# A planned attention and gated feed-forward kernel: GpSimd may take squares and weight sums, the planner's durations are set anew, and every engine gets a new order

## The chip, the cores and the metric

The program runs on one core of a Trainium2 chip. A core has five engines with a queue each: TensorE (PE in the profile, with its weight loads as PEld), VectorE (DVE), ScalarE (ACT), GpSimd (POOL) and SyncE (SP), which here only issues transfers. Each engine takes its instructions strictly in the order in which they were written and starts one only when the semaphores that it waits for have been raised. The metric is the device time of one execution in microseconds (us), median of three: 1039.81 us (1039.11 to 1039.89).

## The reference

Attention with random features, for 8 batches of 8 heads, 576 tokens and 64 dimensions, 128 features, followed by a gated feed-forward layer on 4608 tokens of 512 dimensions, 1536 hidden. Cut to what is computed:

```python
q_s, k_s = q * scale, k * scale
def phi(x):
    h = einsum('bhsd,md->bhsm', x, omega) - sum(x * x, -1, keepdims=True) / 2
    return exp(h - max(h, -1, keepdims=True)) / sqrt(m)
q_p, k_p = phi(q_s), phi(k_s)
kv, z = einsum('bhsm,bhsd->bhmd', k_p, v), sum(k_p, axis=2)
num, den = einsum('bhsm,bhmd->bhsd', q_p, kv), einsum('bhsm,bhm->bhs', q_p, z) + 1e-6
x = (num / den) laid out as (tokens, heads * dims)
out = ((x @ w_a) * (x @ w_b)) @ w_out
```

## The kernel before

Two heads of one batch make a unit; 8 batches of 4 units are 32 units, named in the tiles as batch and pair (`hk_0_1` belongs to batch 0, pair 1). A unit's scores are matmuls of the inputs with omega (L583 for four chunks of 128 tokens, L603 for eight), a row maximum on VectorE (L654, L613), the squares of the inputs and their row sums (`square_sums`: the square at L564, the sum at L569, tiles `natk` and `natq`, result `sq`), two small VectorE instructions that make the bias (L661 and L662) and eight exponentials on ScalarE for each of `hk` and `hq` (L667, L623). In batch 0 the chunks are then transposed on TensorE (L990), multiplied with `kv` (L1013, L1027) and divided (L1032 to L1039) to `x32t` and, turned once more (L1046), to `x`. From batch 1 on the sum over keys, `z`, is added up on GpSimd in six instructions (L829 in `z_sums`), finished on VectorE (L845 to L856), written to memory and read back to all partitions as `zb`; `hq` is divided by it (L895 to L911), turned on VectorE (L918) and through memory, and goes into the numerator `pm` (L950).

The feed-forward layer works block by block, one batch (512 of its tokens) a block, over twelve slices of the hidden dimension. Every value is split into a high and a low part, so a product is three matmuls. In blocks 0 and 1 (`moe_block`) a slice is 12 matmuls into `pa` and 12 into `pb` (L1285), a copy of `pa` to `a` on ScalarE, the product `a` times `pb` on VectorE (L1293), its split into `ghl` (L400 or L402, then L408), and 12 matmuls into the four output banks (L1093). There are two PSUM banks for `pa` and `pb`, so the next slice's `pb` waits for the product of this one. From block 2 on (`moe_block7`, L1383) two slices go together with seven products of half matrices in place of eight. These need sums of quarters of the weights, which `weight_sums` makes once, between the first slice of block 1 and the start of block 2: for each of 6 slice pairs and both weights two adds `wr` (L1317), one subtraction of 128x512 (L1326) and two of 128x256 (L1323, tile `tf`), then their split into `ts` and its transfer to memory. The weights come as 64 bit numbers; three instructions (L450, L452 on ScalarE, L454 on VectorE) and a split (L400 or L402, L408) turn 36 tiles `raw` into high and low parts, in the stretch from about 28 to 171 us.

The order of all work is made by a planner (`Graph`) when the program is built. Each piece of work (`op`) has the engines that may do it, each with a duration in ns, what it reads and writes, and a priority. `run` lays the pieces out in time by these durations, choosing an engine where there is a choice; `dues` works back from the last piece of TensorE to a due time for each; and for each list in `CHOSEN` the layout is made again by due times, with a seed for each 15 us of planned time that shifts due times by random amounts (`shifted`). What is written into each queue is that last order. The durations decide nothing on the chip by themselves; only the order and the choice of engines get into the program. Two rules of the planner's time belong to the change: `PORT` lengthens a VectorE piece that lies beside a GpSimd piece (L284), unless the piece is exempt (`o.port`), and `TURNS` adds a pause where TensorE goes from one kind of matmul to another (`mode`).

In batch 0 the inputs of units 1 to 3 have their squares made on ScalarE (unit 0 has another way, L638 to L643). The weight sums are VectorE's alone.

Of the kernel before, what the change touches and what calls it, by code (L numbers as in the profile page):

```python
# [61 lines left out]
class Graph:  # L62
# [4 lines left out]
    TURNS = {"fr": 190, "rf": 205, "fc": 145, "cf": 205, "rc": 250, "cr": 250}  # L67
# [292 lines left out]
def tile_attention_moe(ctx: ExitStack, tc: tile.TileContext, kqt, kqtt, kqn, kqnt, vx, omst, idn, wab, wout, out):  # L360
# [200 lines left out]
    def square_sums(src, sq, n, nm, pr, b, alloc_sq):  # L561

        for nat, o, part in src:
            s = g.op({"ACT": act(n * D)}, lambda e, nat=nat: nc.scalar.activation(nat.ap[:], nat.ap[:], AF.Square, scale=SQ) if e == "ACT" else  # L564
                     nc.gpsimd.tensor_tensor(nat.ap[:], nat.ap[:], nat.ap[:], op=ALU.mult),
                     r=[(nat, None)], w=[(nat, None)], prio=pr, margin=0 if b < 2 else CFG["LOAD"])
# [1043 lines left out]
```

## Time and profile before

| what | value |
|---|---|
| median of three runs | 1039.81 us |
| the profiled execution's own time | 1038.92 us |
| its span on the core | 1037.1 us |
| PE busy | 1020.0 us (98%) |
| DVE busy | 803.8 us (78%) |
| ACT busy | 635.5 us (61%) |
| POOL busy | 117.2 us (11%) |
| granted clock of TensorE | 0.999 |
| HBM | 302 GB/s over the span |

The share of an engine over the whole span hides stages. In the first 13 us the inputs arrive; until about 50 us the four units of batch 0 run; blocks 0 and 1 of the feed-forward layer with the units of batches 1 to 3 fill the time to 300 us; then the blocks with seven products run to the end, until about 780 us with units beside them. A time of one group of instructions is a mean or a median over the profiled execution. PE counts as busy while a matmul is in its pipeline, so a short pause of TensorE shows in PEld (weight loads) rather than in PE.

### The profile page before, as it was taken

Reading aid. Unit: us, or ns where it says so; the run is one execution under the profiler, and the core shown is the slowest. Engines: PE = TensorE matmul, PEld = TensorE weight load, DVE = VectorE, ACT = ScalarE, POOL = GpSimd, SP = SyncE. Lnnn points to the kernel's source line nnn. Section 1 sums busy time; section 2 is a strip of 40 time slices with the busy share of each in tenths; the row PEclk is TensorE's granted clock in tenths of the full one; section 3 lists DMA queues with packets and bytes.
Section 4 is the critical chain, followed back from the end, with each engine's and each line's share of the span. In section 5 each row is a group of like instructions: output and inputs, shape, how many; then the busy total and the mean of one; then the engine's idle time right before and its main releaser. Section 6 shows DMA issues by size and latency. Waiting matters only on the chain.

```text
span 1037.1 us, 25617 instructions
## 1 busy us (share of the span) xinstructions
PE 1020.0 (98%) x9902; PEld 895.7 (86%) x9902; DVE 803.8 (78%) x1580; ACT 635.5 (61%) x1690; POOL 117.2 (11%) x181
## 2 busy tenths in 40 slices
PE   8899999999999999999999999999999999999998
PEld 6677777777788898989898889988989899999997
DVE  6999999999987687676776868677757467887545
ACT  7998787777676575667556666675555234444322
POOL 0133111111111111110201111111110000000000
PEclk9999999999999999999999999999999999999999
DMA  9977878999889898879898998988798899999991
GB/s 358 335 250 247 291 236 266 323 335 332 292 296 387 301 319 299 319 278 368 283 321 301 340 304 296 363 287 315 249 303 265 267 316 337 334 326 358 338 336 56
DMA packets 123658, 314.39 MB, mean 303 GB/s; under 512 B 17680, under 2 KB 40976, under 8 KB 123536
## 3 DMA queue, kind: packets, MB, share of 16 engines
q1 hardware_dynamic: 122656, 312.10, 86.6%
q8 instruction: 78, 1.28, 0.5%
q10 hardware_dynamic: 880, 0.66, 0.2%
q14 instruction: 44, 0.36, 0.1%
HBM read 255.52 MB, written 57.18 MB: 302 GB/s over the span
## 4 chain that ended last, share of the span: by engine, by line
PE 82%; DVE 12%; ACT 4%; issue 1%; DMA 1%; SPq 0%; DVEq 0%; ACTq 0%
PE p L1383 41%; PE o L1093 19%; PE o_P L1163 5%; PE pa L1285 3%; PE pb L1285 3%; PE pkv L876 3%; PE pm L950 2%; DVE sm L654 2%; PE ppk L603 2%; PE p L603 1%; DVE raw L454 1%; PE p L1163 1%; ACT hq L667 1%; DMA zb<-zdr 1%; ACT hk L667 1%
## 5 line engine op out<-in xcount | busy, mean ns | idle before, releaser
L1093 PE MATMUL o<-wo,ghl 128*128 128x512 f32 x1008 | 263.2, 396 | 0.4 <-DVE ghl L408 0.4
L1093 PEld LDWEIGHTS o<-wo,ghl 128*128 128x128 f32 x1008 | 178.6, 188 | 36.3 <-issue 4.1
L400 ACT COPY c<-p 128x512 f32<-128x512 f32 x150 | 87.4, 583 | 145.7 <-PE p L1383 137.8
L1395 DVE TENSOR_TENSOR c<-p,c 128x512 f32<-128x512 f32 x144 | 98.6, 685 | 71.1 <-PE p L1383 36.4
L1383 PE MATMUL p<-Sa,t 128*128 128x256 f32 x1008 | 133.4, 280 | 0.0
L1383 PEld LDWEIGHTS p<-Sa,t 128*128 128x128 f32 x1008 | 126.2, 188 | 2.3 <-issue 0.2
L829 POOL TENSOR_TENSOR z<-hk 128x256 f32<-128x256 f32 x56 | 48.0, 856 | 601.4 <-ACT hk L623 402.8
L1459 DVE TENSOR_TENSOR c<-c 128x512 f32<-128x512 f32 x82 | 57.8, 707 | 40.1 <-ACT c L400 39.4
L911 ACT ACTIVATE hq<-hq,dn 128x128 f32<-128x128 f32 x224 | 69.3, 390 | 13.5 <-DVE dn L907 13.0
L1285 PE MATMUL pa<-x,wa 128*128 128x512 f32 x288 | 74.4, 400 | 2.1 <-ACT a L400 1.1
L1285 PE MATMUL pb<-x,wb 128*128 128x512 f32 x288 | 72.3, 397 | 1.5 <-DVE a L1293 1.5
L1383 PE MATMUL p<-x,wa 128*128 128x256 f32 x504 | 73.7, 282 | 0.0
L1383 PE MATMUL p<-x,wb 128*128 128x256 f32 x504 | 73.2, 281 | 0.0
L1383 PEld LDWEIGHTS p<-x,wa 128*128 128x128 f32 x504 | 67.2, 188 | 3.3 <-ACT hk L400 0.6
L1383 PE MATMUL p<-Sb,t 128*128 128x256 f32 x504 | 68.4, 283 | 0.0
L1383 PEld LDWEIGHTS p<-x,t 128*128 128x128 f32 x504 | 64.7, 189 | 2.6
L1285 PEld LDWEIGHTS pa<-x,wa 128*128 128x128 f32 x288 | 52.6, 188 | 16.4 <-ACT a L400 1.9
L1383 PE MATMUL p<-Sb,bq 128*128 128x256 f32 x504 | 66.8, 282 | 0.0
L1285 PEld LDWEIGHTS pb<-x,wb 128*128 128x128 f32 x288 | 53.3, 188 | 15.5 <-DVE a L1293 2.8
L1383 PE MATMUL p<-x,t 128*128 128x256 f32 x504 | 66.7, 281 | 0.0
L1383 PEld LDWEIGHTS p<-Sb,bq 128*128 128x128 f32 x504 | 64.3, 189 | 2.4
L1383 PEld LDWEIGHTS p<-x,wb 128*128 128x128 f32 x504 | 65.4, 188 | 0.1
(217 smaller groups left out, 1983.9 us busy)
## 6 DMA issues: line engine op xcount, KB each, us to landing
t<-td SPq DMA_DIRECT2D x168, 512.0 KB
wo<-wod SPq DMA_DIRECT2D x96, 512.0 KB
bq<-bd SPq DMA_DIRECT2D x84, 256.0 KB
qdr<-qd SPq DMA_DIRECT2D x112, 160.0 KB
hq<-qdr SPq DMA_DIRECT2D x28, 640.0 KB
X<-in_kqt_dram SPq DMA_DIRECT2D x30, 512.0 KB
raw<-in_wab_dram SPq DMA_DIRECT2D x24, 512.0 KB
td<-ts SPq DMA_DIRECT2D x24, 512.0 KB
```

The source lines that it names most:

```text
L400: nc.scalar.copy(o(), i())
L603: nc.tensor.matmul(flat[c // 4][w]()[half, c % 4 * M:c % 4 * M + M], x()[rows, c * P + D * t:c * P + D * t + D], om.ap[rows], start=True, ...
L654: g.op({"DVE": dve(4 * M)}, lambda e, w=w, whole=whole: nc.vector.tensor_reduce(sm.ap[:, 0, w, sl], whole(), axis=X, op=ALU.max), r=held[w ...
L829: g.op({"POOL": pool2(n)}, lambda e: nc.gpsimd.tensor_tensor(o(), a(), c(), op=ALU.add), r=r, w=w, alloc=list(al), prio=pri, deps=zload[-1 ...
L876: nc.tensor.matmul(pkv.ap[D * j + d:D * j + d + Q, 0:M], vb.ap[:, vc, d:d + Q], c(), start=(n == 0), stop=(n == 4))
L911: g.op({"ACT": 392}, lambda e, c=c, src=src: nc.scalar.activation(hq.ap[:, c], src(), AF.Copy, scale=dn.ap[:, c:c + 1]), r=[sd, (dn, None) ...
L1093: nc.tensor.matmul(po.ap[:], ghl.ap[:, gi, t * P:(t + 1) * P], wo.ap[:, wi], start=(n == 0 and i == 0), stop=(n == NF - 1 and i == 2))
L1163: nc.tensor.matmul(pb.ap[:, t], A[0](ai)[:, t * P:(t + 1) * P], W[0](wi), start=begin and t == j == 0, stop=stop and t == 1 and j == 2)
L1285: nc.tensor.matmul(pb.ap[:], wt.ap[:, wi, c], xs[c].at(xi), start=(c == 0 and i == 0), stop=(c == NC4 - 1 and i == 2))
L1383: nc.tensor.matmul(pb.ap[:, w], W[w][0](wi, c), X[0](xi, c), start=fresh and n == w == 0, stop=n == 5, skip_group_check=True)
L1395: g.op({"DVE": dve(SM)}, lambda e: nc.vector.tensor_tensor(o.ap[:, q], pb.ap[:], C[y[0]].ap[:, y[1]], op=ALU.add), r=[(pb, 0), (pb, 1), (C ...
L1459: g.op({"DVE": dve(SM)}, lambda e, c=C[k]: nc.vector.tensor_tensor(c.ap[:, :, 1], c.ap[:, :, 1], c.ap[:, :, 0], op=ALU.mult), r=part, w=pa ...
```

## The change

`square_sums` lets GpSimd make the square in batch 0; where it does, the factor 0.5/8 that ScalarE puts into the square is applied by one more small VectorE instruction after the row sum. `weight_sums` lets GpSimd make each of the five sums. The other edits are to the planner's durations: `PORT` goes from 0.5 to 0.4, pieces that read one tensor or reduce are exempt from it (`port=False`), the pauses in `TURNS` become shorter and get a kind `h` for the two small matmul groups of `tok_tail`, whose durations go from 2200 to 1200 and from 1100 to 610, and the two instructions of the division there become one piece. `CHOSEN` holds another list of seeds, 17 long instead of 8: seeds now act in planned time from 15 to 30 us, 195 to 210 us and 240 to 255 us.

```diff
-    TURNS = {"fr": 190, "rf": 205, "fc": 145, "cf": 205, "rc": 250, "cr": 250}
+    TURNS = {"fr": 90, "rf": 150, "fc": 90, "cf": 145, "rc": 170, "cr": 170, "fh": 95, "hf": 125, "rh": 170, "hr": 125, "hc": 150, "ch": 150}
...
-        o.port = not any(b.ring in ("at", "ab", "o") for b, _ in r)
+        o.port = port and not any(b.ring in ("at", "ab", "o") for b, _ in r)
+        if not o.port and "ACT" in eng and any(b.ring in ("at", "ab", "o") for b, _ in r):
+            o.any = eng = dict(eng, ACT=eng["ACT"] - 30)
...
-            s = g.op({"ACT": act(n * D)}, lambda e, nat=nat: nc.scalar.activation(nat.ap[:], nat.ap[:], AF.Square, scale=SQ) if e == "ACT" else
-                     nc.gpsimd.tensor_tensor(nat.ap[:], nat.ap[:], nat.ap[:], op=ALU.mult),
+            s = g.op({"ACT": act(n * D) + 25, **({"POOL": pool2(n * D)} if b == 0 else {})}, lambda e, nat=nat: nc.scalar.activation(nat.ap[:], nat.ap[:], AF.Square, scale=SQ) if e == "ACT" else
+                 nc.gpsimd.tensor_tensor(nat.ap[:], nat.ap[:], nat.ap[:], op=ALU.mult),
...
                 if "POOL" in s.eng:
-                    nc.gpsimd.tensor_scalar(o(), o(), SQ2, 0.0, op0=ALU.mult, op1=ALU.add)
+                    nc.vector.tensor_scalar(o(), o(), SQ2, None, op0=ALU.mult)
...
-            g.op({"DVE": dve(SM)}, lambda e, k=k, v=v: nc.vector.tensor_tensor(wr.ap[:, k], v(0), v(1), op=ALU.add),
+            g.op({"DVE": dve(SM), "POOL": pool2(SM)}, lambda e, k=k, v=v: ENG[e].tensor_tensor(wr.ap[:, k], v(0), v(1), op=ALU.add),
...
-            g.op({"DVE": dve(HM)}, lambda e: nc.vector.tensor_tensor(t[k](), x(), y(), op=ALU.subtract),
+            g.op({"DVE": dve(HM), "POOL": pool2(HM)}, lambda e: ENG[e].tensor_tensor(t[k](), x(), y(), op=ALU.subtract),
...
-        g.op({"DVE": dve(SM)}, lambda e: nc.vector.tensor_tensor(tf.ap[:, 1:3], wr.ap[:, 1].rearrange("p (h n) -> p h n", n=HM), wr.ap[:, :, 0:HM],
+        g.op({"DVE": dve(SM), "POOL": pool2(SM)}, lambda e: ENG[e].tensor_tensor(tf.ap[:, 1:3], wr.ap[:, 1].rearrange("p (h n) -> p h n", n=HM), wr.ap[:, :, 0:HM],
```

Counted over the built programs, TensorE has the same instructions in another order, and goes from one kind of matmul to another 170 times, before 168 times. All six squares of batch 0 go from ScalarE to GpSimd, with six small VectorE instructions (L573 in the changed kernel) more. Of the 60 weight sums 24 go to GpSimd: nine `wr`, three `tf` of 128x512 and twelve `tf` of 128x256. Of the casts and copies that either engine may make, VectorE has 79 instead of 83.

Three places in the order matter. The first is ScalarE's queue from the last exponentials of unit 0 to the first ones of unit 1 (`hk_0_1`, `hq_0_1`). Before:

```order
L667 ACTIVATE hq_0_0_182<-ppq_0_04_240,sm_0_0_183 128x128 x4
L564 ACTIVATE natk_0_1_157<-natk_0_1_157 128x512
L667 ACTIVATE htk_0_0_210<-ppke_0_00_208,sme_0_0_212 128x128
L400 COPY kvz_0_0_331<-pkv_0_0_330 128x132
L667 ACTIVATE htk_0_0_210<-ppke_0_00_208,sme_0_0_212 128x128
L564 ACTIVATE natq_0_1_159<-natq_0_1_159 128x512
L400 COPY qT_0_0_320<-pq_0_02_366 128x384
L667 ACTIVATE htq_0_0_211<-ppqe_0_00_209,sme_0_0_212 128x128 x3
L564 ACTIVATE natk_0_2_165<-natk_0_2_165 128x512
L564 ACTIVATE natq_0_2_167<-natq_0_2_167 128x512
L564 ACTIVATE natk_0_3_173<-natk_0_3_173 128x512
L667 ACTIVATE hq_0_1_296<-ppq_0_14_375,sm_0_1_297 128x128 x4
```

The same stretch of ScalarE's queue in the changed kernel:

```order
L669 ACTIVATE hq_0_0_182<-ppq_0_04_240,sm_0_0_183 128x128 x4
L669 ACTIVATE htk_0_0_210<-ppke_0_00_208,sme_0_0_212 128x128 x3
L402 COPY kvz_0_0_340<-pkv_0_0_339 128x132
L669 ACTIVATE hk_0_1_296<-ppk_0_10_294,sm_0_1_298 128x128 x2
L402 COPY qT_0_0_324<-pq_0_02_380 128x384
L669 ACTIVATE hk_0_1_296<-ppk_0_10_294,sm_0_1_298 128x128
L669 ACTIVATE hq_0_1_297<-ppq_0_10_295,sm_0_1_298 128x128
```

Five squares stood ahead of unit 1's first exponential; now none does, and it follows the copy of `kvz` directly. The second place is GpSimd's queue from its start. Before:

```order
L424 MEMSET zw_70 128x32
L1018 MEMSET tails_0_1_483 64x128
L1018 MEMSET tails_0_2_730 64x128
L1018 MEMSET tails_0_3_840 64x128
L829 ISA
L829 TENSOR_TENSOR z2_1_0_993<-hk_1_0_913 128x256
```

GpSimd's queue from its start in the changed kernel:

```order
L426 MEMSET zw_70 128x32
L567 ISA
L567 TENSOR_TENSOR natk_0_1_157<-natk_0_1_157 128x512
L567 TENSOR_TENSOR natq_0_1_159<-natq_0_1_159 128x512
L567 TENSOR_TENSOR natk_0_2_165<-natk_0_2_165 128x512
L567 TENSOR_TENSOR natq_0_2_167<-natq_0_2_167 128x512
L567 TENSOR_TENSOR natk_0_3_173<-natk_0_3_173 128x512
L567 TENSOR_TENSOR natq_0_3_175<-natq_0_3_175 128x512
L1020 MEMSET tails_0_1_564 64x128
```

The six squares, and with them the configuring instruction that precedes GpSimd's first `TENSOR_TENSOR` (shown as `ISA`), moved ahead of everything that waits for batch 0's results. The third place is GpSimd's queue at the first slice of block 1, between the `z` sums of units 2_1 and 2_2, in the changed kernel (before, the `z` sums follow each other there):

```order
L831 TENSOR_TENSOR zs_2_1_2458<-z2_2_1_2457 128x128
L831 TENSOR_TENSOR zs_2_1_2458<-zs_2_1_2458,htk2_2145 64x128
L1328 TENSOR_TENSOR tf00_2721<-wr00_2636 128x512
L1325 TENSOR_TENSOR tf00_2721<-wr00_2636,tf00_2721 128x256
L1319 TENSOR_TENSOR wr01_2760<-wb1_1099 128x512
L831 TENSOR_TENSOR z2_2_2_2809<-hk_2_2_2614 128x256
L831 TENSOR_TENSOR zs_2_2_2810<-z2_2_2_2809 128x128
```

Three weight sums now stand ahead of unit 2_2's `z` sum in the same queue.

## Rows read from the trace of the kernel before

**Rows 1.** Busy time by stage: the stretch, its length, busy us and instructions (x) of each engine, TensorE's granted clock, the busy share of the transfer engines, GB/s.

```profile
0.00:13.00 13.00, 11.51 (x193) 8.58 (x195) 6.35 (x16) 7.33 (x21) 0.94 (x10) 1.00 0.84 304
13.00:46.00 33.00, 26.80 (x552) 21.99 (x549) 30.26 (x81) 32.81 (x99) 1.30 (x3) 1.00 0.98 378
...
60.00:165.00 105.00, 103.61 (x903) 79.61 (x896) 103.72 (x212) 91.42 (x242) 22.67 (x25) 1.00 0.77 253
165.00:300.00 135.00, 133.15 (x1144) 102.81 (x1143) 130.55 (x252) 97.53 (x265) 25.23 (x36) 1.00 0.93 319
300.00:780.00 480.00, 480.00 (x4958) 429.10 (x4959) 348.19 (x661) 303.42 (x841) 61.87 (x102) 1.00 0.89 311
```

**Rows 2.** What TensorE's weight loads waited for from 165 to 300 us, longest first: who waits, for whom, us in total, times, longest.

```profile
PEld pkv L952 <- issue: 3.6, 12, 0.3
PEld pa L1285 <- ACT a L400: 1.9, 2, 1.3
PEld pkv L876 <- issue: 1.8, 5, 0.4
PEld pb L1285 <- DVE a L1293: 0.9, 1, 0.9
```

**Rows 3.** The timeline of ScalarE, 13.6 to 18 us and at the last split of batch 0's `x`: start us, length us, engine, line, operation, tiles.

```profile
13.62 0.77 ACT L564 ACTIVATE natk<-natk 128x512 f32<-128x512 f32 x1
...
16.44 0.83 ACT L564 ACTIVATE natk<-natk 128x512 f32<-128x512 f32 x1
16.95 0.83 ACT L564 ACTIVATE natq<-natq 128x512 f32<-128x512 f32 x1
17.48 0.83 ACT L564 ACTIVATE natk<-natk 128x512 f32<-128x512 f32 x1
18.00 1.33 ACT L667 ACTIVATE hq<-ppq,sm 128x128 f32<-128x128 f32 x4
19.02 1.35 ACT L667 ACTIVATE hk<-ppk,sm 128x128 f32<-128x128 f32 x4
...
45.71 0.59 ACT L400 CAST x<-px 128x512 fp32r<-128x512 f32 x1
```

**Rows 4.** The timeline of VectorE around unit 1's first row sum, with the idle time before an instruction and who ended it; then around the first product of block 0 (`a<-pb,a`).

```profile
11.18 0.69 DVE L654 TENSOR_REDUCE sm<-ppk 128x4 f32<-128x512 f32 x1 [0.75 <-PE ppq L583]
14.42 0.69 DVE L569 TENSOR_REDUCE sq<-natk 128x8 f32<-128x512 f32 x1 [1.49 <-ACT natk L564]
...
54.38 0.68 DVE L1293 TENSOR_TENSOR a<-pb,a 128x512 f32<-128x512 f32 x1
...
58.53 0.43 DVE L845 STREAM_TRANSPOSE z<-zs 128x256 f32<-128x256 f32 x1
59.00 0.42 DVE L846 TENSOR_REDUCE zq<-z 128x8 f32<-128x256 f32 x1
```

**Rows 5.** The timeline of TensorE at the second slice of block 0.

```profile
51.61 3.04 PE L1285 MATMUL pa<-x,wa 128*128 128x512 f32 x12
55.11 2.35 PE L1285 MATMUL pb<-x,wb 128*128 128x512 f32 x9 [0.45 <-DVE a L1293]
57.38 1.08 PE L876 MATMUL pkv<-hk,v 128*32 128x128 f32 x32
```

**Rows 6.** Small VectorE instructions, grouped over the whole run: busy us, mean ns of one, idle before.

```profile
L906 DVE TENSOR_SCALAR dn<-dn 128x9 f32<-128x9 f32 x28 | 5.7, 203 | 0.0
```

**Rows 7.** The weight sums on VectorE, grouped by line from 165 to 300 us, with the same columns; then each line's shortest, median and longest duration in ns over the run.

```profile
L1323 DVE TENSOR_TENSOR tf<-wr,tf 128x256 f32<-128x256 f32 x22 | 10.1, 458 | 0.2
L1317 DVE TENSOR_TENSOR wr<-wa 128x512 f32<-128x512 f32 x12 | 9.2, 774 | 0.1
L1326 DVE TENSOR_TENSOR tf<-wr 128x512 f32<-128x512 f32 x12 | 9.1, 762 | 0.1
L1317 DVE TENSOR_TENSOR wr<-wb 128x512 f32<-128x512 f32 x12 | 8.5, 708 | 0.0
...
L1317 DVE TENSOR_TENSOR wr<-wa x12: 676/690/1133, 165.1 to 284.5; 128x512 f32<-128x512 f32 x12
L1326 DVE TENSOR_TENSOR tf<-wr x12: 636/688/1242, 175.2 to 297.1; 128x512 f32<-128x512 f32 x12
L1323 DVE TENSOR_TENSOR tf<-wr,tf x24: 371/418/971, 176.3 to 303.7; 128x256 f32<-128x256 f32 x24
```

**Rows 8.** GpSimd's additions, shortest, median and longest duration in ns, first and last start in us; its configuring instruction; and who let its first addition go.

```profile
L829 POOL TENSOR_TENSOR z<-hk x56: 722/742/2672, 49.5 to 770.5; 128x256 f32<-128x256 f32 x56
L829 POOL TENSOR_TENSOR zs<-z x56: 452/464/1979, 50.8 to 771.6; 128x128 f32<-128x128 f32 x56
L829 POOLq MODIFY_POOL_CONFIG  x2: 3/3/3, 39.0 to 39.0; - x2
```

**Rows 9.** The timeline of GpSimd at the same place.

```profile
1.43 0.13 POOL L424 MEMSET zw<- 128x32 f32 x1
...
49.54 1.15 POOL L829 TENSOR_TENSOR z<-hk 128x256 f32<-128x256 f32 x1 [10.49 <-ACT hk L667]
51.63 1.07 POOL L829 TENSOR_TENSOR z<-hk 128x256 f32<-128x256 f32 x1
```

**Rows 10.** The chain that ended last, one of its longest pieces: start us, length us, what.

```profile
116.35 6.75 DMA zb<-zdr
```

**Rows 11.** The weight loads of the first group of matmuls of block 2, in ns, and their first and last start in us.

```profile
L1383 PEld LDWEIGHTS p<-x,wa x504: 186/188/193, 299.9 to 1011.7; 128*128 128x128 f32 x168
```

More of the change, by code (lines that the diff above doesn't have):

```diff
@@ L79, in buf, with op @@
         return b
-    def op(self, eng, fn, r=(), w=(), prio=0, alloc=(), deps=(), margin=0, nbytes=0, at=0, land=0, late=(), fill=False, mode="f"):
+    def op(self, eng, fn, r=(), w=(), prio=0, alloc=(), deps=(), margin=0, nbytes=0, at=0, land=0, late=(), fill=False, mode="f", port=True):
         o = Op()
@@ L570, in total @@
                 if "POOL" in s.eng:
-                    nc.gpsimd.tensor_scalar(o(), o(), SQ2, 0.0, op0=ALU.mult, op1=ALU.add)
-            g.op({"DVE": dve(n * D)}, total, r=[(nat, None)], w=[(sq, part)], alloc=[sq] if part in (0, None) else [], prio=pr)
+                    nc.vector.tensor_scalar(o(), o(), SQ2, None, op0=ALU.mult)
+            g.op({"DVE": dve(n * D)}, total, r=[(nat, None)], w=[(sq, part)], alloc=[sq] if part in (0, None) else [], prio=pr, port=False)
     def four(nm, b, pri, x, xdep, dst, c0, sm, sq, al, deps, mg, more):
@@ L613, in eight @@
             g.op({"DVE": dve(8 * M)}, lambda e, w=w, to=to, at=at: nc.vector.tensor_reduce(sm.ap[:, 0, w], to.ap[:, at:at + 8], axis=X, op=ALU.max),
-                 r=cols[w], w=[(sm, (0, w))], prio=pri + w)
+                 r=cols[w], w=[(sm, (0, w))], prio=pri + w, port=False)
         def biases(e):
@@ L900, in divide @@
             prod().rearrange("p (j c m) -> p j c m", j=2, m=M), hq.ap[:, 0:8].rearrange("p (j c) m -> p j c m", j=2),
-            zb.ap[:].unsqueeze(2).to_broadcast([P, 2, 4, M]), op=ALU.mult), r=[(hq, c) for c in range(8)] + [(zb, None)], w=[(qd, None)], prio=pri)
+            zb.ap[:].unsqueeze(2).to_broadcast([P, 2, 4, M]), op=ALU.mult), r=[(hq, c) for c in range(8)] + [(zb, None)], w=[(qd, None)], prio=pri, port=False)
         g.op({"DVE": dve(8 * M)}, lambda e: nc.vector.tensor_reduce(dn.ap[:, 0:8], prod().rearrange("p (c m) -> p c m", m=M), axis=X, op=ALU.add),
-             r=[(qd, None)], w=[(dn, 0)], prio=pri)
+             r=[(qd, None)], w=[(dn, 0)], prio=pri, port=False)
         def inv(e):
@@ L918, in turn @@
         g.op({"DVE": dve(NCH * M)}, lambda e: nc.vector.transpose(qd.ap[:, :, 0:NCH], hq.ap[:, 0:NCH].rearrange("p c (j r) -> p j c r", r=32)),
-             r=[(hq, c) for c in range(NCH)], w=[(qd, 0)], prio=pr + 110)
+             r=[(hq, c) for c in range(NCH)], w=[(qd, 0)], prio=pr + 110, port=False)
         if u == NU - 1:
@@ L1013, in kvmm @@
                         nc.tensor.matmul(pf[t:t + D, at:at + VW], c()[:, t:t + D], vf[:, vc * VW:vc * VW + VW], start=(n == 0), stop=(n == 4))
-        g.op({"PE": mm4(10, VW)}, kvmm, r=[(vb, None), (h[0], None), (he[0], hp)], w=[(pkv, None)], alloc=[pkv, kvz], prio=pr + 100, margin=mg)
+        g.op({"PE": 1200}, kvmm, r=[(vb, None), (h[0], None), (he[0], hp)], w=[(pkv, None)], alloc=[pkv, kvz], prio=pr + 100, margin=mg, mode="h")
         g.op({"ACT": act(2 * VW)}, copier(lambda: kvz.ap[:], lambda: pkv.ap[:, :, 0:VW]), r=[(pkv, None)], w=[(kvz, None)], prio=pr + 100)
```

30 lines of the change are left out of this document (15 added, 15 removed).

## Prediction

> **What bounds the kernel now.** I read the table of stages first [rows 1], then the waits of TensorE, then single timelines. In the table the reader should compare, row by row, busy time with the length of the stretch. From 13 to 46 us ScalarE is the full engine (32.81 of 33.00 us) with VectorE behind it (30.26). From 60 to 165 us TensorE (103.61 of 105.00) and VectorE (103.72) are both full, and from 165 to 300 us TensorE has 133.15 of 135.00 and VectorE 130.55. From 300 us TensorE is busy in all 480.00 of 480.00 us while VectorE is at 348.19. No edit reaches the work after 300 us other than by order, so a gain must come from pauses of TensorE before that. PE's busy time hides short pauses, since a matmul counts while it is in its pipeline; so I looked at what the weight loads wait for [rows 2]. From 165 to 300 us the longest rows name TensorE itself ("issue", the turn from one kind of matmul to another, 3.6 and 1.8 us); waits that name another engine are 1.9 us for the copies of `pa` and 0.9 us for the products of VectorE. That is the first lesson of this profile: VectorE is 97% busy there, yet TensorE rarely waits for it. My ceiling for the stretch is the sum of the rows that name other engines, 1.9 + 0.9 = 2.8 us, and, since smaller rows stand below those shown, an estimated 6 us.
>
> **The squares.** Six squares leave ScalarE. They start 0.52 us apart (16.44, 16.95, 17.48 [rows 3]), so 6 x 0.52 = 3.1 us come free on ScalarE in its full stretch. But the new order also fills that room. Counted ahead of the last copy of batch 0's `x`, at 45.71 [rows 3], two squares for later units have left as well (8 x 0.52 = 4.2 us in all), and eight exponentials of unit 1_0 have come, four of which take 1.02 us by the starts at 18.00 and 19.02 [rows 3]: +2.0 us. One weight cast and one copy more, against a step on a weight and small copies less, I put at +0.4. That is -1.8 us on ScalarE ahead of that copy. VectorE gets six `TENSOR_SCALAR`, about 0.20 us each by a like instruction (203 ns [rows 6]): +1.2 us, part of it in its own idle time, which is 1.49 us ahead of the first row sum, waiting for the square, and 0.75 us for `ppq` [rows 4]. On GpSimd a square of 128x512 does not occur before. Its additions take 742 ns for 256 elements and 464 ns for 128 [rows 8]: 278 ns for each 128, so 742 + 2 x 278 = 1.30 us as an estimate, and 6 x 1.30 = 7.8 us for all. The engine is idle then, after 1.43 us [rows 9], and the inputs are what it waits for. The first square on ScalarE ran at 13.62 us [rows 3]; if GpSimd starts only then, two squares end at 13.62 + 2 x 1.30 = 16.2 us, then come two row sums (0.69 each [rows 4]) and the bias, and unit 1's first exponential runs at about 17.7 us where it ran at 18.00. If it starts when the tile has arrived, some 4 us sooner (about when the tiles behind the row maximum at 11.18 [rows 4] must have come), it is at about 14. So this edit is no loss on this path, and a lead of at most 4 us, which the full ScalarE passes on in part.
>
> What VectorE meets before block 0's first product (54.38 [rows 4]) is the other side. The new order puts pieces of unit 1_0 ahead of it: a transpose and a reduction of `z` (0.43 + 0.42 [rows 4]), two row maxima (0.69 each [rows 4]) and four small instructions (0.20 each [rows 6]); the weight steps and casts that come and go about cancel. With the 1.2 us above that is 1.2 + 0.85 + 1.4 + 0.8 = +4.2 us, and +3.0 us on TensorE's own queue, among it the `pkv` of 1.08 us [rows 5], moved forward and so not lost. The second slice's `pb` waits for the first product, 0.45 us before [rows 5]. With TensorE's additions of 3.0 us the two delays nearly meet: 4.2 - 3.0 = 1.2 us at most is left of the difference, and the shorter idle time on VectorE takes some of that. For the start I take a gain of 1.0 us: 1.8 us less on ScalarE, less up to 0.8 us of delay on VectorE. The bounds are a gain of 1.8 + 1.49 = 3.3 us (ScalarE's room and VectorE's idle time both arrive) and a loss of 4.2 - 1.49 = 2.7 us (VectorE's additions delay the first product in full, less the idle time that goes away).
>
> **The weight sums.** 24 sums leave VectorE. By line [rows 7]: 3 `wr` from `wa` at 0.774, 6 from `wb` at 0.708, 3 `tf` of 128x512 at 0.762 and 12 of 128x256 at 0.458: 2.32 + 4.25 + 2.29 + 5.50 = 14.4 us. GpSimd pays 12 x 1.30 + 12 x 0.742 = 24.5 us for them and has room: it is busy 25.23 of 135 us [rows 1]. Part comes back as interference. The same lines show it: means against medians are 774 to 690, 762 to 688 and 458 to 418 ns, and the longest 1133, 1242 and 971 ns [rows 7]. That loses 12 x 0.084 + 12 x 0.074 + 22 x 0.040 = 2.8 us on these lines; other VectorE work with two tensors from SBUF I take as about the same again, so some 5 to 6 us for 25.23 us of GpSimd, 0.2 us for each. 24.5 x 0.2 = 5 us given back; bounds 0 and all 24.5. VectorE is relieved by 14.4 - 5 = 9 us of 130.55.
>
> [...]
>
> What the 9 us are worth is read from TensorE's waits, not from VectorE. The 0.9 us for the products and some of the 1.9 us for the copies [rows 2] can shrink, with the unnamed small ones perhaps half of 6 us. The new order has two turns more (170 for 168), 12 turns cost 3.6 us [rows 2], so 0.3 us each: +0.6 us. And GpSimd's queue now holds three weight sums (1.30 + 0.74 + 1.30 = 3.3 us) ahead of unit 2_2's `z`; behind it stand the `z` sums, VectorE's transpose, the transfer of `zb` (6.75 us on the chain that ended last [rows 10]) and the numerator. I take a gain of 1.5 us here: half of 6, less 0.6 for turns and 0.9 for such delays. The bounds are a gain of 5 us and a loss of 3 us. From 60 to 165 us nothing of the change's work stands except order, with both engines full: 0, bounds 1.5 either way.
>
> **The sum.** -1.0 + 0 - 1.5 = -2.5 us. Against the profiled execution's 1038.92 us (its span of 1037.1 and 1.8 around it) this gives 1036.4; the median of the three runs is 0.9 above that execution, so the forecast is 1039.8 - 2.5 = 1037.3 us.
>
> **Rivals.**
> First rival, nothing: TensorE is bound by its own work and turns throughout, so less work on the others only makes their idle time longer. For it: the largest waits name "issue" [rows 2], and 97% on VectorE costs TensorE 0.9 us by name. Against it: ScalarE's 32.81 of 33.00 us at the start, where TensorE really waits. Time: 1039.81 less 1.0 for the start plus 0.6 for turns, 1039.5 us.
>
> Second rival, slower: GpSimd's queue becomes the late one. A `z` sum that had an idle engine now stands behind up to 3.3 us of weight sums, each waiting itself for a cast of weights, and behind `z` everything up to the numerator of that unit. It decides once the delay is longer than the room that `zb` has ahead of its numerator; if it strikes in one unit of block 1 with the full 3.3 us, and nothing is gained, the time is 1039.8 + 3.3 = 1043.1 us. For it: `zb` is on the chain that ended last before [rows 10]. Against it: GpSimd is idle four fifths of the stretch, and later units can make up for it.
>
> Third rival, slower at the start: GpSimd is late for its first call. Before, its configuring instruction stood at 39.0 us, 3 ns long [rows 8], and the first addition ran at once when its operand came at 49.54, in 1.15 us against 1.07 for the next one [rows 9]. The 10.49 us of waiting ahead of it could hide a preparation; in the changed kernel the queue has its squares right behind it, and a preparation that ends after 13.62 us would hold all unit 1's bias. A delay of 4 us, from 13.62 to 17.6 us, at the full ScalarE gives 1039.8 + 4 = 1043.8 us, within 1 either way. [...]
>
> **How the numbers follow.** What a measurement of this kernel can tell from no change is 0.2%, 2.1 us. The forecast, relief that reaches TensorE, has 0.45; its own range is 1034 to 1038.5. The first rival has 0.33, the second 0.17, the third 0.05. The low end takes the gains of 3.3 and 5 us at three quarters (6.2 us): 1033.5; the high end is the second rival, 1043.0, with the third just outside. A gain above 2.1 us has 0.45, no change 0.33, slower 0.17 + 0.05 = 0.22.
>
> **What would show it.** Right: the last `x` copy on ScalarE before 45.71, unit 1's first exponential before 18.00, no 1.49 us idle ahead of the first row sum, GpSimd's 128x512 at about 1.30 us, VectorE's busy time from 165 to 300 us down by about 9 from 130.55, and block 2's first weight load earlier than 299.9 us [rows 11] by 2 to 3 us. Wrong: VectorE's remaining sums with means near 1.0 us (full contention), `pm` or `pd` of 2_2 waiting for `zb`, a first square on GpSimd after 14 us, or a start of block 2 at the old place with less idle time nowhere but on VectorE.

## The result: slower by 0.83%

The changed kernel takes 1047.47 us (median of five runs, 1046.99 to 1049.62) against 1039.69 (1039.08 to 1039.89), a ratio over all executions of 1.0083 with an interval of 1.0070 to 1.0097 (the two medians are 7.8 us, or 0.75%, apart). The forecast was 1037.3, its range ended at 1043.0. The profiled execution took 1049.14 us with a span of 1047.3, so its parts add up to more than the 7.8 us between the medians. One execution of e2, below, took 2551.85 us and is left out of e2's numbers.

The table of busy time by stage, as in [rows 1], after the change; behind it the row from 46 to 60 us of the kernel before, which [rows 1] leaves out:

```profile
0.00:13.00 13.00, 12.00 (x199) 8.85 (x201) 6.84 (x19) 7.06 (x20) 2.97 (x12) 1.00 0.85 304
13.00:46.00 33.00, 28.95 (x569) 22.98 (x569) 31.03 (x83) 30.24 (x98) 6.65 (x10) 0.99 0.92 354
46.00:60.00 14.00, 12.53 (x110) 8.65 (x104) 12.54 (x28) 12.73 (x35) 2.35 (x5) 0.78 0.72 237
60.00:165.00 105.00, 103.53 (x918) 79.23 (x922) 102.83 (x206) 92.35 (x239) 23.75 (x30) 1.00 0.78 259
165.00:300.00 135.00, 129.83 (x1042) 100.76 (x1035) 126.69 (x220) 91.58 (x244) 47.86 (x49) 0.99 0.89 306
300.00:780.00 480.00, 479.48 (x4937) 427.63 (x4936) 348.24 (x661) 303.87 (x845) 64.19 (x105) 1.00 0.90 310
```

```profile
46.00:60.00 14.00, 12.90 (x130) 9.27 (x132) 13.90 (x26) 12.13 (x33) 5.23 (x6) 1.00 0.86 269
```

ScalarE is relieved from 13 to 46 us as forecast (30.24 for 32.81), GpSimd takes the sums from 165 to 300 us (47.86 for 25.23). But VectorE's 126.69 for 130.55 is 3.9 us less, not 9, and TensorE has lost 3.3 us of busy time there. In the column before the last two something is new: a granted clock of 0.78 from 46 to 60 us, where it was 1.00 before. Cut into pieces of 2 us (length, PE busy, clock, share of the transfer engines, GB/s):

```profile
42.00:44.00 2.00, 0.92 (x3) 1.00 0.84 323
44.00:46.00 2.00, 1.87 (x34) 0.84 0.06 18
46.00:48.00 2.00, 1.31 (x10) 0.50 0.21 63
48.00:50.00 2.00, 1.96 (x5) 0.50 0.18 68
50.00:52.00 2.00, 2.00 (x20) 0.50 0.77 240
52.00:54.00 2.00, 2.00 (x37) 0.95 1.01 287
```

TensorE stood still for 1.1 us of the 2 us from 42 to 44, in two pauses, worked again from 43.6 us, and from about 45.4 to 52 us runs at a granted clock of 0.50. The clock falls again behind a pause of 1.68 us that ends at 229.53 us:

```profile
230.00:232.00 2.00, 2.00 (x28) 0.50 0.76 227
232.00:234.00 2.00, 2.00 (x8) 0.72 0.64 152
```

The clock is not the main loss, though: one of the five executions of the changed kernel had a mean clock of 1.000 and still took 1046.99 us, and in the trace of e2 below, which has the same order, the clock never falls at these places (1.00 from 36 to 60 and from 165 to 300 us) while it is 8.3 us late at the end.

To see where time is lost although the order differs, I gave each matmul the mean distance to the next that its kind has in the trace of before, and read when each run had done so much of this work. The sums of two orders differ by some tenths at a place. Columns: us of work done, the time in before, and how much later the others are.

| work | before | after | e1 | e2 | e4 | e5 | e6 | e7 | e8 | e16 | e17 |
|---|---|---|---|---|---|---|---|---|---|---|---|
| 40 | 42.7 | -2.0 | -1.0 | -0.1 | +0.7 | +1.3 | -1.1 | +1.3 | -1.8 | +1.3 | +1.2 |
| 46 | 50.8 | +2.4 | +3.2 | +2.3 | +0.7 | +1.2 | +3.3 | +1.3 | +0.4 | +6.7 | +1.2 |
| 50 | 55.7 | +1.6 | +2.5 | +1.6 | +0.7 | +1.2 | +2.5 | +1.3 | -0.2 | +5.9 | +1.2 |
| 60 | 66.0 | +2.4 | +3.2 | +2.8 | +0.7 | +1.2 | +3.3 | +1.3 | +0.9 | +5.9 | +1.2 |
| 80 | 87.9 | +2.3 | +3.5 | +2.8 | +0.7 | +8.8 | +4.8 | +1.3 | +3.0 | +5.6 | +1.2 |
| 180 | 191.0 | +2.7 | +4.0 | +3.0 | +0.7 | +8.7 | +5.0 | +11.3 | +3.7 | +6.1 | +1.3 |
| 200 | 212.1 | +1.7 | +3.0 | +2.0 | +1.5 | +8.1 | +5.0 | +10.2 | +3.9 | +6.1 | +1.0 |
| 300 | 315.2 | +8.1 | +7.1 | +8.1 | +4.6 | +14.1 | +4.7 | +16.7 | +3.6 | +6.1 | +1.3 |
| 500 | 517.8 | +7.7 | +6.9 | +7.7 | +4.5 | +13.5 | +4.9 | +16.1 | +3.7 | +6.2 | +1.4 |
| 600 | 618.7 | +9.3 | +8.0 | +8.0 | +4.5 | +13.8 | +4.9 | +17.3 | +3.8 | +6.2 | +1.3 |
| 980 | 999.6 | +9.6 | +8.3 | +8.3 | +4.4 | +13.6 | +5.0 | +17.0 | +3.9 | +6.2 | +1.3 |

The runs differ from their first instructions on (at 6 us of work the changed kernel is 0.3 us late, e1 0.6, e2, e16 and e17 1.4, e8 0.4), so a column is read downwards. The change is 2.0 us ahead after 40 us of work, loses 4.4 until 60, keeps about level until 200, and loses 6.4 between 200 and 300. So of the 10 us by which this execution is longer the larger part is lost late. Another 1.6 us go between 500 and 600 in this execution; e2, which has the same order there, does not lose them.

Block 2's first weight load, for [rows 11], came 5.6 us later than before:

```profile
L1385 PEld LDWEIGHTS p<-x,wa x504: 186/188/193, 305.5 to 1021.3; 128*128 128x128 f32 x168
```

What TensorE waited for from 165 to 300 us, the longest rows that name another engine (as [rows 2]; `PE` and `PEld` of `ppqb` are the same wait):

```profile
PEld ppqb L605 <- DVE a L1295: 1.9, 1, 1.9
PEld pm L952 <- ACT kl L402: 1.9, 2, 1.2
PE ppqb L605 <- DVE a L1295: 1.7, 1, 1.7
PEld ppq L605 <- DVE st L552: 1.7, 1, 1.7
```

The single waits for VectorE are longer than the 0.9 us that [rows 2] showed for it. The timelines around the first two (TensorE, ScalarE, VectorE, GpSimd, in pieces):

```profile
221.07 1.06 PE L952 MATMUL pm<-hq,kl 128*32 128x512 f32 x8 [0.94 <-ACT kl L402]
...
229.53 0.34 PE L605 MATMUL ppqb<-om,X 64*64 64x128 f32 x1 [1.68 <-DVE a L1295]
...
219.38 0.62 ACT L402 CAST ts<-tf 128x512 fp32r<-128x512 f32 x1 [1.28 <-POOL tf L1325]
220.20 0.62 ACT L402 CAST ts<-tf 128x512 fp32r<-128x512 f32 x1 [0.20 <-POOL tf L1325]
220.72 0.29 ACT L402 COPY kl<-hq 128x128 f32<-128x128 f32 x1
...
220.74 1.26 DVE L908 TENSOR_SCALAR dn<-dn 128x9 f32<-128x9 f32 x1
...
227.08 1.79 DVE L410 TENSOR_TENSOR ts<-tf,ts 128x512 fp32r<-128x512 f32 x1
228.79 0.68 DVE L1295 TENSOR_TENSOR a<-pb,a 128x512 f32<-128x512 f32 x1
...
217.75 2.41 POOL L1325 TENSOR_TENSOR tf<-wr,tf 128x256 f32<-128x256 f32 x2
220.25 1.73 POOL L1319 TENSOR_TENSOR wr<-wa 128x512 f32<-128x512 f32 x1
...
226.58 1.74 POOL L1319 TENSOR_TENSOR wr<-wb 128x512 f32<-128x512 f32 x1 [4.60 <-DVE tf L1325]
```

Two ways from GpSimd to TensorE stand here. At 219 us the copy `kl` that `pm` needs is queued on ScalarE behind two casts that wait for GpSimd's `tf`. Then lay the VectorE rows beside the GpSimd rows: a `TENSOR_SCALAR` of 128x9, 203 ns in [rows 6], takes 1.26 us, and a split that takes 0.69 elsewhere takes 1.79. The first ends when GpSimd's addition ends (220.25 + 1.73 = 221.98 us), the second 0.55 us after one ends (226.58 + 1.74 = 228.32). The second stands ahead of the product `a`, which frees the bank that TensorE's `ppqb` wants.

### The profile page after: what moved, and what is told of

Its sections match the earlier page's. It is cut to its first block, busy times and chain, and to the rows that moved or that the text cites. A ratio compares the mean times of both kernels' runs of the same rounds, so it can differ in the third digit from the quotient of the medians.

```text
span 1047.3 us, 25649 instructions
## 1 busy us (share of the span) xinstructions
PE 1028.0 (98%) x9902; PEld 900.9 (86%) x9902; DVE 803.0 (77%) x1558; ACT 634.8 (61%) x1688; POOL 149.3 (14%) x211
## 3 DMA queue, kind: packets, MB, share of 16 engines
q8 instruction: 78, 1.28, 0.5%
## 4 chain that ended last, share of the span: by engine, by line
PE 81%; DVE 12%; ACT 3%; DMA 2%; issue 1%; SPq 0%; POOL 0%; DVEq 0%; ACTq 0%; POOLq 0%
PE p L1385 39%; PE o L1095 19%; PE o_P L1165 5%; PE pb L1287 3%; PE pkv L878 3%; PE pa L1287 3%; PE pm L952 2%; PE ppk L605 1%; PE p L605 1%; DVE raw L456 1%; DMA natk<-in_kqn_dram 1%; DVE ts L410 1%; PE ppk L585 1%; PE p L1165 1%; DVE sm L656 1%
## 5 line engine op out<-in xcount | busy, mean ns | idle before, releaser
L1095 PE MATMUL o<-wo,ghl 128*128 128x512 f32 x1008 | 265.9, 397 | 0.1
L1287 PEld LDWEIGHTS pa<-x,wa 128*128 128x128 f32 x288 | 53.5, 189 | 16.1 <-ACT x L402 1.2
```

The costliest lines, as they stand in the source:

```text
L1095: nc.tensor.matmul(po.ap[:], ghl.ap[:, gi, t * P:(t + 1) * P], wo.ap[:, wi], start=(n == 0 and i == 0), stop=(n == NF - 1 and i == 2))
L1287: nc.tensor.matmul(pb.ap[:], wt.ap[:, wi, c], xs[c].at(xi), start=(c == 0 and i == 0), stop=(c == NC4 - 1 and i == 2))
```

## Experiments

**Who does the work, in one order.** The emission loop is the only place changed: an instruction keeps its place among all others and goes to another engine. e1 puts the 24 sums of the changed kernel back on VectorE, e2 the six squares back on ScalarE, e3 both; what is left of the change in e3 is the order, with the choice between ScalarE and VectorE that came with it for casts and copies.

```diff
         for o in order:
+            if o.prio == 500000 and "POOL" in o.eng:   # e1, e3
+                o.eng = {"DVE": 0}
+            if "POOL" in o.eng and "ACT" in o.any:     # e2, e3
+                o.eng = {"ACT": 0}
```

e4 is the kernel before with the same 24 sums on GpSimd (`ENG[e]` in the three lines as in the change):

```diff
+        sums = [o for o in g.ops if o.prio == 500000]
+        for k in (2, 4, 13, 15, 25, 38, 39, 40, 48, 61,
+                  63, 64, 72, 76, 84, 86, 87, 88, 99, 108, 111, 132, 133, 135):
+            sums[k].eng = {"POOL": 0}
```

> The changed kernel's order, with the 24 weight sums put back on VectorE at the places where they stood; squares stay on GpSimd. Theory P (ports): GpSimd's weight sums hold up VectorE instructions that TensorE waits for (the dn step of 1.26 us at 220.7, the split of 1.79 us ahead of a product at 227.1), and of the 8 us these cost about 3 to 4: 1043.5 to 1045, TensorE's waits of 1.21 us at 219.9 and 1.95 us at 227.6 gone, VectorE 4 us busier from 156 to 305 us net (14.3 more, 10.1 of excess gone). Theory O (order): the new order of the queues costs the time, whoever makes the sums: 1046.5 to 1048.5.

> The changed kernel's order, with the six squares of batch 0 put back on ScalarE at their places (and the six small VectorE instructions gone); weight sums stay on GpSimd. Theory S (squares): GpSimd's squares at the start cause the 4 to 5 us by which the first product of block 0 is late (59.3 against 54.4): 1043 to 1044.5. Theory O (order): the squares are a help, ScalarE gets 6 x 0.52 = 3.1 us more in its full stretch: 1047.5 to 1050.

> The changed kernel's order with both back: 24 sums on VectorE, six squares on ScalarE, so that only order and the choice between ScalarE and VectorE differ from the kernel before. Theory O (order alone): 1047 to 1050. Theory P (ports): 1044 to 1046. If the engines alone were the cause: 1039 to 1041.

> The kernel before, its order kept, with the same 24 weight sums on GpSimd at their places. Theory P (ports): VectorE is held up for 0.35 us for each us of GpSimd's 28 us (10 us), 14.3 us leave it, but single waits of 1 to 2 us land ahead of TensorE: 1041.5 to 1045. Theory O (order): the sums as such cost nothing, VectorE is relieved: 1038.5 to 1040.5.

Measured: e1 1046.23 us, 1.0056 of before (1.0040 to 1.0073); e2 1048.03, 1.0080 (1.0064 to 1.0097); e3 1047.40, 1.0073 (1.0058 to 1.0088); e4 1042.92, 1.0031 (1.0019 to 1.0043). With sums and squares back where they were, e3 loses 7.9 us, as much as the changed kernel: the order, with that choice in it, is the main cause. In the order of before, the sums on GpSimd cost 3.4 us by themselves, though by the prediction's count they take 14.4 us from VectorE. In the new order they cost 1.2 us between the medians, inside the spread; of the three waits above two are still there in e1, and with the same figures in e3:

```profile
PEld ppqb L605 <- DVE a L1295: 1.7, 1, 1.7
PEld ppq L605 <- DVE st L552: 1.7, 1, 1.7
```

One place of e4, VectorE and GpSimd:

```profile
214.54 3.20 DVE L895 CUSTOM_DVE_ANT_0 zero<-htq,zb 64x128 bf16<-64x128 f32 x1
...
214.87 0.73 POOL L1323 TENSOR_TENSOR tf<-wr,tf 128x256 f32<-128x256 f32 x1
215.56 0.72 POOL L829 TENSOR_TENSOR z<-hk 128x256 f32<-128x256 f32 x1
216.25 1.28 POOL L1317 TENSOR_TENSOR wr<-wa 128x512 f32<-128x512 f32 x1
```

An instruction whose median is 0.29 us takes 3.20, until about when the third of these GpSimd additions, which follow each other without a pause, ends at 217.53. The weight sums among them (L1323, L1317) are what the edit put there.

**Which part of the order.** Both orders, with their engines, stand in a table here, and one is followed up to the start of a slice of the feed-forward layer, the other from there (what the first has done is left out of the second):

```diff
-    order = g.plan()
...
+    order = []
+    for row in zlib.decompress(base64.b85decode(TABLE)).decode().split(";"):
+        n, e, *slots = row.split(",")
...
```

> The order (and engines) of the kernel before up to the start of block 0's fourth slice (about 80 us), the changed kernel's from there to the end. Theory E (early): the start costs the time (the first product 4.9 us late, clock down after it): 1040 to 1042. Theory L (late): the loss comes after 200 us: 1045 to 1047.5. Both halves by the lost time read from the two traces (4 us by the start, 4 later, of 8): 1043 to 1044.

> The reverse: the changed kernel's order up to block 0's fourth slice, the order and engines of the kernel before from there. Theory E (early): 1045 to 1047.5. Theory L (late): 1040 to 1042. Both: 1043 to 1044.

> The order of the kernel before up to the start of block 1 (about 175 us), the changed kernel's from there: all weight sums of the changed kernel, none of its start. Theory L (late): 1043.5 to 1047; theory E (early): 1040 to 1042.

> The changed kernel's order up to the start of block 1, the order and engines of the kernel before from there: the squares and the new start, no weight sum on GpSimd. Theory E (early): 1043 to 1047; theory L (late): 1039.5 to 1041.5.

Measured: e5 1052.64 (ratio 1.0126, 1.0111 to 1.0141), e6 1044.33 (1.0053, 1.0034 to 1.0072), e7 1053.76 (1.0136, 1.0119 to 1.0153), e8 1042.98 (1.0035, 1.0022 to 1.0049). e5 and e7 are slower than either parent, and outside all that was expected: the joint itself loses time (in the table e5 is 8.8 us late right behind it, e7 11.3), and the mean granted clock falls there, to 0.91 from 60 to 100 us in e5 and to 0.92 from 165 to 230 us in e7, 1.00 before in both stretches. What comes behind the joint can still be read: from 80 to 300 us of work e5 goes from 8.8 to 14.1, from 180 to 300 e7 goes from 11.3 to 16.7, and the changed kernel from 2.3 to 8.1; e6 and e8, which follow the old order there, stay level. So the new order, with its sums on GpSimd, loses some 5 to 6 us late. By the medians e6 and e8 are 5.0 and 3.6 us slower than before; part of that can be lost at the joint, since the two parts add up to more than the 7.8 us of the whole.

e9 is the kernel before with only the six squares on GpSimd (the same override, on the six operations):

> The kernel before, its order kept, with only the six squares of batch 0 on GpSimd (and the six small VectorE instructions). Theory G (the squares are a gain by themselves: after 43 us of TensorE's work the kernels with squares on GpSimd were 1.0 to 2.0 us ahead of the kernel before, those without at -0.1): 1037.5 to 1039. Theory H (ScalarE's room is not used in this order): 1039 to 1040.5.

Measured: 1040.42 us, 1.0011 (1.0001 to 1.0021), no gain. What the changed kernel is ahead at 40 us of work is mostly its order's doing: from 6 to 40 us of work it gains 2.3 us, and e2, with the squares on ScalarE, 1.5.

**Mending the new order by hand.** e10 moves the divisions and splits of batch 0's units 2 and 3 up in the queues, behind what they need; e11 does this for all VectorE steps that read PSUM between about 195 and 320 us, with the sums on VectorE; e12 is e10 up to block 1 and the old order from there. `psum` holds the steps that read a PSUM tile, `held[b]` the tile that had the place of `b` before; e11 has `"DVE" in o.eng and 195000 < o.start < 320000` for the condition on `prio`.

```diff
...
+    for o in order[:]:
+        if o in psum and 2150 <= o.prio <= 3160 and o.prio % 1000 >= 130:
+            users = [u for b in o.alloc if held[b] for u in held[b].users]
+            t = max(x.end + (150 if "PE" in x.eng else 70) for x in [*o.deps, *users])
+            if t < o.start:
+                o.end -= o.start - t
+                o.start = t
+    order.sort(key=lambda o: (o.start, o.n))
```

> The changed kernel, in which only the steps that read PSUM in the divisions and the splits of batch 0's units 2 and 3 are moved up in the queues of VectorE and ScalarE, to behind what they need (x_0_2's split, rd and x32t of unit 3 ahead of weight steps). Theory Q (queued late: weight steps and unit 1_0 stand ahead of what TensorE waits for at 41.5 to 48 us; 2.2 us, and 2 more where the clock then falls): 1043.5 to 1045.5, first product of block 0 2 to 4 us earlier than 59.3. Theory D (VectorE and ScalarE have too much to do ahead of it, whatever the order): 1046.5 to 1048.

> As e1 (changed order, sums on VectorE), and every VectorE step that reads PSUM is moved up to behind what it needs, in the order of about 195 to 320 us. Theory Q (in the changed order VectorE's sums stand ahead of products and of the steps that free a PSUM bank: waits of 1.8, 1.0 and 1.9 us at 227.6, 266.6 and 293.1 us in e1): 1041.5 to 1044 against 1046.2. Theory D (VectorE is too full there): 1045.5 to 1048.

> The order of e10 up to the start of block 1 (about 175 us), the order and engines of the kernel before from there, so squares on GpSimd, mended start, no sums on GpSimd. Theory Q: e8's 1043.0 less 2 to 4: 1039 to 1041. Theory D: 1042.5 to 1044.

Measured: e10 1050.86 (1.0109, 1.0094 to 1.0124), e11 1049.28 (1.0091, 1.0076 to 1.0106), e12 1044.87 (1.0053, 1.0038 to 1.0068). All three went the wrong way, and e10 and e11 are slower even than theory D expected. Moving the steps up this way mends nothing; that another place for them would, the runs do not exclude. In e11 TensorE lost 0.53 us at the product's wait of 227 us, where e1 lost 1.48, but another of 1.12 us came at 294, beside the one for `st`, which stayed; behind the two the clock fell to 0.57 from 296 to 300 us:

```profile
294.02 0.43 PE L605 MATMUL ppk<-om,X 64*64 64x128 f32 x2 [1.12 <-ACT k L402]
295.46 0.32 PE L605 MATMUL ppq<-om,X 64*64 64x128 f32 x1 [1.01 <-DVE st L552]
```

In e10 the steps that moved up delayed the bias of unit 1_0, and TensorE's `ppke` waited 2.4 us for the exponentials behind it. e13 therefore puts the turn `px` ahead of `ppke`, e14 moves `ppke` behind block 0's first `pb`, as in the kernel before, e15 does both:

```diff
+        if 2150 <= o.prio <= 3160 and o.prio % 1000 >= 130 and (o in psum or o.prio % 1000 >= 150 and "PE" in o.eng):   # e13, e15
...
+        if o.prio == 4005 and "PE" in o.eng and o.start < 50000:          # e14, e15
+            t = 48250
```

> e10 with one step more: the last turn of batch 0 (px and pt of unit 3) goes ahead of the scores ppke of unit 1_0 in TensorE's queue too. Theory B (the bank: ppke waits for the exponentials and holds up px and all behind it): x_0_3's split 2 to 4 us earlier than in e10, less of the clock lost: 1045.5 to 1048 against e10's 1050.9. Theory D (VectorE and ScalarE have too much to do ahead of it): 1050 to 1052.

> The changed kernel, in which only ppke of unit 1_0, and whatever needs it, moves back behind the first matmuls of block 0's pb, as in the kernel before; no step is pulled up. Theory B (the bank): TensorE has its turn px right behind the division, no stop at ppke: 1043.5 to 1046 against 1047.5, the clock stays up. Theory D: 1047 to 1050.

> e13 and e14 together: division and splits of batch 0 pulled up, px ahead, ppke behind pb. Theory B: 1043 to 1045.5, the first product of block 0 at 55 to 57 us against 59.3. Theory D: 1047 to 1051.

Measured: 1050.36 (1.0105, 1.0090 to 1.0120), 1052.77 (1.0128, 1.0111 to 1.0144) and 1051.47 (1.0121, 1.0105 to 1.0137). Theory B falls as well, and e14 and e15 are again slower than theory D expected. In e13's profiled execution the clock stayed at 1.00 from 36 to 66 us, and its time, 1049.73 us, is as high as e10's 1049.86.

**VectorE's work by itself, and the short sums by themselves.** What the changed kernel, e10 and e13 to e15 share is how much VectorE has to do ahead of block 0's first product. The stretch up to that product, before and then after the change (length, PE, PEld, VectorE, ScalarE, GpSimd):

```profile
0.00:54.38 54.38, 46.04 (x796) 36.21 (x796) 44.95 (x111) 47.14 (x134) 6.04 (x17) 1.00 0.93 342
```

```profile
0.00:59.29 59.29, 53.49 (x868) 40.48 (x868) 49.70 (x126) 49.33 (x148) 11.46 (x25) 0.94 0.86 316
```

111 instructions in 44.95 us against 126 in 49.70: 4.75 us more work, and the product starts 4.91 us later. e16 puts such an amount into the kernel before and changes nothing else; e17 is e4 with the twelve sums of 128x256 alone.

```diff
...
         for o in order:
+            if o is division:      # e16: the first step of unit 3's division
+                for _ in range(14):
+                    nc.vector.tensor_reduce(spare_out[:], ident.ap[:], axis=X, op=ALU.add)
```

> The kernel before with 14 row sums of 128x128 on VectorE, whose result nobody uses, ahead of the division of batch 0's unit 3 (some 4 us of work, at about 42.9 us). Theory V (VectorE's extra work ahead of the first product is what the changed start costs): the first product about 4 us later than 54.4, the time up by 2 to 4.5 us, TensorE's clock down for a while in some runs: 1041.5 to 1044. Theory D2 (VectorE has slack there, TensorE waits for ScalarE): 1039.5 to 1040.8.

> e4 with only the twelve 128x256 sums on GpSimd (12 x 0.458 = 5.5 us off VectorE), the twelve of 128x512 stay on VectorE. If the loss goes with the length of GpSimd's instruction (blocked for 0.74 at most instead of 1.3 to 1.7 us): 1039.3 to 1041. If it goes with the number, half of e4's 3.4: 1041 to 1042.

Measured: e16 1044.85 us, 1.0048 (1.0031 to 1.0064); e17 1039.80, 1.0001 (0.9992 to 1.0011). The timelines of e16, VectorE and TensorE, and its clock:

```profile
44.16 4.45 DVE L1543 TENSOR_REDUCE spare_out<-ident 128x1 f32<-128x128 f32 x14
48.53 0.15 DVE L1032 TENSOR_SCALAR rd<-pn 128x5 f32<-128x5 f32 x1
...
60.00 0.68 DVE L1293 TENSOR_TENSOR a<-pb,a 128x512 f32<-128x512 f32 x1
...
50.43 1.12 PE L1046 MATMUL px<-ident,x32t 128*128 128x128 f32 x4 [5.72 <-DVE x32t L1035]
```

```profile
42.00:48.00 6.00, 2.71 (x74) 0.99 0.94 334
48.00:54.00 6.00, 3.57 (x11) 0.50 0.33 118
54.00:60.00 6.00, 6.00 (x52) 0.94 0.81 242
```

4.45 us of work whose result nobody uses cost 5.0 us between the medians, with the fall of the clock that came too: a wait of TensorE of 1.37 us for `x32t` became one of 5.72 us, and the first product came 5.6 us later. Theory D2, that VectorE has slack there, falls. The time is above the 1044 us at which theory V ended, and e16 shows the price only for work directly ahead of a step that TensorE waits for. That the changed start loses by its 4.75 us, which stand elsewhere, it does not show. There the price can be read at the first product itself, from TensorE's row behind it in the changed kernel and in e8, which has the same order up to 175 us (before, the wait was 0.45 us [rows 5]):

```profile
60.03 0.97 PE L1287 MATMUL pb<-x,wb 128*128 128x512 f32 x3 [0.77 <-DVE a L1295]
...
58.51 0.96 PE L1288 MATMUL pb<-x,wb 128*128 128x512 f32 x3 [1.07 <-DVE a L1296]
```

In e8 the clock stayed up (1.00 from 36 to 60 us), VectorE did 127 instructions in 49.83 us ahead of the product, and it came at 57.78 us, 3.4 later than before. TensorE lost only 0.3 to 0.6 us more by the late product than before.

Twelve short sums (11 us of GpSimd's time) cost nothing, so e4's 3.4 us need the twelve of 128x512, by themselves or beside the short ones; the twelve alone were not run.

## Why the prediction was wrong

*The step that failed: what a new order costs.* The prediction priced the new order at 0.6 us for two more turns and 0.9 us for delays in GpSimd's queue, and otherwise let it only shorten waits. e3, with sums and squares back on their engines, loses 7.9 us. The parts by stage follow.

*ScalarE and the squares: right, but hardly a gain.* The squares run at 1.04 us each (1.30 estimated), the first as soon as its tile is there, and unit 1's first exponential at 14.78 us, near the "about 14" of the better case ([rows 3] had 18.00):

```profile
9.56 1.04 POOL L567 TENSOR_TENSOR natk<-natk 128x512 f32<-128x512 f32 x1 [8.01 <-DMA natk<-in_kqn_dram]
10.56 1.04 POOL L567 TENSOR_TENSOR natq<-natq 128x512 f32<-128x512 f32 x1
...
14.78 0.62 ACT L669 ACTIVATE hk<-ppk,sm 128x128 f32<-128x128 f32 x2
```

The first row sum follows at 10.64 us without the 1.49 us of idle time of [rows 4]. From 6 to 40 us of work the kernel gains 2.3 us, but with the squares back on ScalarE (e2) it gains 1.5 as well, and the squares alone (e9) gain nothing. The third rival fell with the same rows: the configuration came at 1.5 us and no delay shows at 9.56; the 8.01 us of waiting ahead of it could still have covered one.

*The start: a gain of 1.0 forecast, a loss measured.* The count of +4.2 us on VectorE ahead of the first product was right (4.75 measured), and the step "with TensorE's additions of 3.0 us the two delays nearly meet" held where it can be read: the product came 3.4 us (e8) to 4.9 us later, and `pb` waited 0.3 to 0.6 us longer for it. What failed is that the lead arrives. From 40 to 60 us of work e8, with the clock up, loses 2.7 us, e2 2.9 and the changed kernel 4.4. TensorE's pauses there are in part other ones than before (at `pt`, 0.73 us in the changed kernel and 1.20 in e8 and e2, and longer ones at the first `pa` of block 0, which waits for the splits of `x`, 1.15 us in all in the changed kernel, 1.26 in e8 and 1.32 in e2, 1.00 before); they name part of the loss, and the rest of it stays open.

*The clock: not in the sum at all.* The 4.4 us of the changed kernel against the 2.7 and 2.9 of e8 and e2, whose clock was up there (1.00 from 36 to 60 us), put the fall at 45 us at some 1.6 us, an estimate. (In e8 the clock fell later, to a mean of 0.96 from 60 to 100 us, and it lost 2.1 us between 60 and 80 us of work.) With the execution at a clock of 1.000 that took 1046.99 us, this is the smaller part of the loss.

*The give-back: mis-sized.* I took 0.2 us for each us of GpSimd. Adding up by how much VectorE's instructions beside GpSimd exceed the median of their form between 156 and 310 us gives 17.7 us in the changed kernel and 5.1 in e1, which has the same order without the sums: 12.6 us for 27.8 us of GpSimd, 0.45 for each, so 12.6 of the 14.4 us saved came back. In e4 it is 14.9 against 6.5 in before, 0.30; in e17 7.3 against 6.5 for 11.1 us, 0.07. That VectorE's other work with two tensors from SBUF loses as much as the lines of the sums was my estimate, and no run shows it apart; the 0.45 is over all of VectorE's work. The sum of 14.4 - 5 = 9 us of relief should have been about 2. The old trace held additions with medians of 0.46 and 0.74 us [rows 8], and their rate was carried over to instructions twice as long (shortest, median, longest in ns):

```profile
L1319 POOL TENSOR_TENSOR wr<-wb x6: 1294/1522/1750, 183.5 to 282.5; 128x512 f32<-128x512 f32 x6
L1319 POOL TENSOR_TENSOR wr<-wa x3: 1279/1675/1731, 206.7 to 234.5; 128x512 f32<-128x512 f32 x3
```

VectorE's row at 220.74 us ends with GpSimd's addition (222.00 and 221.98 us), the one at 227.08 ends 0.55 us after one. In e1, which has the same order with the sums on VectorE, the same two steps, at 222.27 and 227.50 us, take 0.15 and 0.68 us in place of 1.26 and 1.79. GpSimd's additions are longer at such places too, 1.73 us for one whose shortest was 1.28. The full 24.5 us, the prediction's bound, were not reached: 12.6 us were lost beside 27.8 us of GpSimd.

*What the late relief is worth: sign wrong, and the largest miss.* The rule that it is read from TensorE's waits was right, and the 3.9 us by which VectorE was less busy indeed bought nothing. But a gain of 1.5 us was forecast, because I let the new order only shorten waits. It made new ones, 1.9, 1.9 and 1.7 us by the rows above, and two of the three stay with the sums on VectorE (in e1 and e3 `ppqb` waits 1.7 us for the product and `ppq` 1.7 for `st`): these two are most of what the order loses here. The loss from 200 to 300 us of work is 6.4 us in the changed kernel, 6.1 in e2, whose clock stayed up, and 4.1 in e1: about 4 for the order, 2 for the sums. How to order the steps without these waits is not settled: e11 moved them and lost more.

*The second rival, GpSimd's queue late for `z`, fell at its place:* unit 2_2's `z` sum started at 185.1 us, before at 186.1. The loss came through VectorE instead. *From 60 to 165 us:* 0 was forecast, and from 60 to 180 us of work the difference goes from 2.4 to 2.7. *Two slips of arithmetic:* the first rival's 1039.81 - 1.0 + 0.6 is 1039.4, not 1039.5, and the forecast's own range, up to 1038.5, holds gains from 1.3 us on, so its whole chance of 0.45 could not go to a gain above 2.1 us. Neither bears on the miss.

## What to carry to other kernels

Before giving GpSimd work that VectorE has, look at how long one of its instructions is: here twelve sums of 0.74 us went through at no cost (e17, 1039.80 against 1039.88 us), and with twelve more of 1.3 to 1.7 us the loss was more than the relief was worth (e4, 3.4 us slower); the rows show short steps held by them, though no run counts what those holds cost. In e16 4.45 us of VectorE's work cost 5.0 us directly ahead of a step that TensorE waits for, with the fall of the clock that came too; where TensorE had other work to do, a first product that came 4.9 us later cost it 0.3 us. So price a new order by the waits that it can make, not by busy time. And an order that was found by a search is hard to mend by hand: of five local repairs here (e10, e11, e13 to e15), each argued from a row of waits, all lost time.

## What the runs showed that was not expected

Behind pauses, TensorE ran for several us at a granted clock of 0.50 at a time when it had work: from 45.4 to 52 us after the change, behind pauses of 0.80 and 0.35 us, and from 50.4 to 54 in e16, behind one of 5.72. Such a pause did not always bring it: e1 waited 1.48 us at 229 us, e13 2.3 us at `pt`, and the clock stayed at 1.00. A VectorE instruction of 64x128 with a median of 0.29 us took 3.20 us in e4, through three GpSimd additions in a row. And joining two good orders at one point costs more than either differs from the other: 8.8 and 11.3 us at the joints of e5 and e7, almost nothing at that of e8.
